# Two pairs of v times p in one TensorE visit, with five p buffers, a first softmax in halves, one W_out piece decoded later, and a new order

## The chip, the core and the metric

The kernel runs on one core of a Trainium2 chip. Its engines are TensorE (PE, with PEld for weight loads), VectorE (DVE), ScalarE (ACT), GpSimd (POOL) and SyncE (SP, which issues the DMAs); SBUF is the working memory, PSUM has eight banks of 128 x 512 words of 32 bits, which TensorE writes. The metric is the device time of one execution, in microseconds, as the median of several.

## The reference

Block-causal attention over 8 batches x 8 heads x 576 positions x 64, then a two-layer network with a gate on 4608 tokens:

```python
scores = scale * np.matmul(q, k.transpose(0, 1, 3, 2))      # q, k, v: (8, 8, 576, 64)
mask = (pos[:, None] // 64) >= (pos[None, :] // 64)
scores = np.where(mask, scores, -1000000000.0)
scores = scores - np.max(scores, axis=-1, keepdims=True)
attn = np.exp(scores)
attn = attn / (np.sum(attn, axis=-1, keepdims=True) + 1e-09)
x = np.matmul(attn, v)            # heads side by side: (4608, 512)
h = x @ w_in                      # (512, 2048)
g = h * (1.0 / (1.0 + np.exp(-h)))
out = g @ w_out                   # (2048, 512)
```

`w_in` and `w_out` arrive as 64-bit floats. q and k are scaled so that the softmax is not flat.

## The kernel before

**Precision.** A product is made of two parts of each operand, high and low, in the type fp32r: hi times hi, hi times lo and lo times hi. So every operand is split, as a rule by a cast on ScalarE (`hi`) and a subtraction on POOL (`lo`). v times p alone is in plain 32-bit floats.

**Attention.** The first two blocks of 64 queries are done apart at the start: block 0 by `First` (units a and b, four batches each) and block 1 by `Second` (c0 to c3). The other 448 queries of each head are a `Unit`, u0 to u63. A unit loads q and k, splits them (`split_hi`, `split_q`, `split_k`), makes transposed scores in three of four PSUM banks (`scores`, L702, tile S), reduces their maximum across partitions with transposing reductions (`max`, `gather`, `top`, `spread`, `wide`), subtracts it (`sub`, L745, L748, L739, tile T), takes the exponential (`exp`, into one of three p buffers), sums (`add`, `sums`), and each odd unit multiplies v and p for itself and its even mate at once, two halves of the array side by side (`pv`, L805, tile U, one PSUM bank of its own). `mult` (L809, tile xu) divides by the sums and `x_hi`, `x_lo` split the result.

**Network.** As soon as a batch's x is there, W_in's product runs in pieces (`ffn1`, L1031, tile h), whose results are kept (`keep`) and saved to DRAM (`save`). The 64 visits of `scores` and the visits of `pv` lie between these pieces. W_in's and W_out's 64-bit words are turned to 32 bits on the chip by integer operations (`rebias` on ScalarE, `sign` on POOL, `bits` on VectorE; 16 pieces w0 to w15 and o0 to o15). W_out's pieces pass in pairs through one buffer (`Turned`, t0 to t7), which forms seven combinations for a product of seven instead of eight multiplications: `x` makes sums, `hi` and `lo` split. t0 to t2 are made early and lie in a pool of their own ("ta"), t3 to t7 after the last attention unit. Then the second product goes over 18 blocks of 256 tokens with four items each (i0 to i71): `load`, `silu`, `x`, `hi`, `lo`, `prod` (L1108), and `keep`, `add` (L1143), `store` of each block's output (y0 to y17).

**Order.** No scheduler works here. A text of tokens, `ORDER`, such as `u23.pv` or `ffn`, is gone through from the first to the last, and each token's method issues its instructions to the queues of their engines, which run in that order, each instruction waiting for the semaphores of what it needs. `warm:10` issues ten matmuls of zeros.

Of the kernel before, what the change touches and what calls it, by code (L numbers as in the profile page):

```python
# [68 lines left out]
a.load b.load a.load_v w0.load b.load_v warm:10 a.scores w1.load w2.load a.max:0 a.sub:0 warm:3 b.scores c0.load a.max:1 a.sub:1  # L69
b.max:0 a.exp w3.load b.max:1 w4.load a.sum w0.rebias w0.sign w5.load b.sub:0 w6.load a.norm b.sub:1 w7.load w0.bits:0 b.exp  # L70
w0.bits:2 o1.load w1.rebias w1.sign warm:30 a.turn:0 b.sum w0.hi a.turn:1 a.back:0 w8.load w0.lo a.back:1 w1.bits:0 w2.rebias
warm:2 a.pv o0.load w1.bits:2 b.norm a.hi:0 c0.load_v a.hi:1 a.lo:0 w1.hi a.lo:1 w2.sign warm:7 b.turn:0 w3.rebias c3.load
c0.scores:0 b.back:0 b.turn:1 w5.rebias w1.lo w2.bits:0 w4.rebias ffn c0.max:0 b.back:1 w3.sign w2.bits:2 c0.exp:0 w9.load b.pv
w3.bits:0 c0.scores:1 w10.load all.mask b.hi:0 w3.bits:2 b.hi:1 ffn w2.hi c0.max:1 c3.load_v w3.hi w2.lo b.lo:0 c0.exp:1 b.lo:1
w4.bits:0 w3.lo ffn c0.sum w6.rebias c1.load w4.bits:1 w7.rebias c0.norm w4.bits:2 ffn keep w11.load w8.rebias w5.bits:0 w4.hi
save c0.turn:0 w5.bits:1 keep w4.lo c3.scores:0 w12.load c0.back:0 w5.bits:2 o1.rebias c0.turn:1 c3.max:0 w5.hi ffn save w6.bits:0
c0.back:1 w5.lo c3.exp:0 w6.bits:1 w13.load c0.pv w6.bits:2 c3.scores:1 c0.hi c1.load_v w7.bits:0 w6.hi ffn c0.lo w10.rebias
w14.load w6.lo c3.max:1 w9.rebias w7.bits:1 c3.exp:1 c1.scores:0 w7.bits:2 ffn c1.max:0 w15.load keep c3.sum c1.exp:0 save
w8.bits:0 c3.norm ffn w8.bits:1 w7.hi w8.bits:2 c1.scores:1 keep w7.lo w9.bits:0 c3.turn:0 w11.rebias save c1.max:1 w8.hi c2.load
ffn w9.bits:1 c3.back:0 w8.lo c1.exp:1 w9.bits:2 c3.turn:1 ffn w10.bits:0 c3.back:1 c1.sum w10.bits:1 w9.hi c1.norm c3.pv keep  # L80
w10.bits:2 w12.rebias ffn save w11.bits:0 w10.hi w9.lo w13.rebias w11.bits:1 c1.turn:0 o0.rebias w11.bits:2 ffn w10.lo c1.back:0
w12.bits:0 w11.hi w14.rebias c1.turn:1 w12.bits:1 w11.lo ffn c1.back:1 w12.bits:2 keep w13.bits:0 w15.rebias save c1.pv w12.hi
w13.bits:1 ffn w12.lo c1.hi c2.load_v w13.bits:2 c1.lo w13.hi c2.scores:0 w14.bits:0 keep w13.lo w14.bits:1 save ffn u0.load
c2.max:0 w14.bits:2 c2.exp:0 ffn w15.bits:0 w15.bits:1 w14.hi c2.scores:1 w15.bits:2 keep w14.lo ffn save c2.max:1 w15.hi u1.load
o0.bits:0 w15.lo all.staged c2.exp:1 ffn o0.bits:1 o0.bits:2 u0.split_hi ffn c2.sum o2.load o1.bits:0 c2.norm keep o1.bits:1
t0.hi:0 ffn save o1.bits:2 u0.split_q t0.hi:1 o3.load c2.turn:0 keep ffn u0.split_k c2.back:0 save c2.turn:1 ffn u2.load t0.x:0
c2.back:1 t0.x:1 c2.pv t0.hi:2 keep t0.x:2 u0.load_v ffn c2.hi save t0.lo:0 c3.hi u2.load_v c2.lo t0.hi:3 u3.load_v t0.lo:2 ffn
c3.lo u1.load_v t0.lo:3 u0.scores keep u0.max:0 t0.lo:1 save u0.max:1 ffn u1.split_hi u0.max:2 o2.rebias ffn u1.split_q u0.gather
o2.bits:0 o3.rebias u1.split_k u0.top ffn o2.bits:1 u0.spread u0.wide keep u3.load ffn u0.sub:0 u0.sub:1 save u0.exp:0 u1.scores
u0.sub:2 u0.exp:1 u0.exp:2 u1.max:0 ffn u1.max:1 u2.split_hi u0.add:0 u1.max:2 keep ffn u2.split_q u0.sums:0 u1.gather save  # L90
o2.bits:2 u0.add:1 u1.top ffn u1.spread o4.load o3.bits:0 u2.split_k u1.wide keep t1.hi:0 ffn u0.sums:1 save u1.sub:0 u4.load
t1.lo:0 u1.sub:1 u1.exp:0 u2.scores keep u1.sub:2 u1.exp:1 save u2.max:0 ffn u1.exp:2 u2.max:1 u3.split_hi u1.add:0 u2.max:2 u1.pv
# [344 lines left out]
def attn_ffn(ctx: ExitStack, tc: tile.TileContext, qk, v, qk0, v0, qk1, v1, w_in, w_out, out):  # L437
# [53 lines left out]
    class Weights:  # L491
# [21 lines left out]
        def rebias(u):  # L513
            if u.signed:
                u.w = bank((1, "C")[u.i])
            else:
# [1 line left out]
            nc.scalar.activation(u.w, u.word(1).bitcast(F32), AF.Copy, scale=REBIAS)
# [730 lines left out]
```

## Time and profile before

| | |
|---|---|
| three runs | 998.52, 998.63, 999.65 us; median 998.63 |
| profiled execution | 999.48 us, span of the instructions 997.8 us |
| granted TensorE clock | 1.00 in the whole span |
| busy share of the span | PE 99%, PEld 89%, DVE 77%, ACT 69%, POOL 62% |
| 16 DMA engines | 51.9% by the hardware queue |

The span is what lies between the first and the last instruction; the execution's time has 1.68 us more around it. In the rows of the trace the columns are the start, the duration, the engine, the line of the kernel, the operation, output and inputs, shape and number, and in brackets the idle time of the engine just before and what ended it. In a row of a stage they are its bounds, its length, each engine's busy time with the number of instructions in the order PE, PEld, DVE, ACT, POOL, then the granted clock, the DMA engines' share and GB/s. A matmul's duration includes the pipeline, so what it holds TensorE for is the step from its start to the next start.

### The profile page before, as it was taken

The page shows a single profiled execution, that of the slowest core. Times are in us where ns is not written, and L with a number is a line of the kernel's source. Part 1 is how long each engine was busy: PE and PEld are TensorE (multiplying, and loading weights), DVE is VectorE, ACT ScalarE, POOL GpSimd, SP SyncE. Part 2 cuts the span into 40 slices and gives each one's busy share as a digit, 9 for nine tenths or more (in the row PEclk, how much of TensorE's full clock was granted, in tenths as well). Part 3 has the DMA queues.
Part 4 walks back from the last instruction along what each step waited for, and adds up shares of the span by engine and source line. Part 5 has one row for each costly group of instructions (what it writes and reads, how often), then busy time and mean ns, then how long its engine had stood idle before and what let it go on. Part 6 is the DMA issues. An engine that isn't in the chain of part 4 may idle for free. (4 is left out here: it accounts for less than half of the span.)

```text
span 997.8 us, 20716 instructions
## 1 busy us (share of the span) xinstructions
PE 987.2 (99%) x6936; PEld 888.9 (89%) x6936; DVE 768.4 (77%) x1969; ACT 692.4 (69%) x1555; POOL 616.0 (62%) x722
## 2 busy tenths in 40 slices
PE   8999999999999999999999999999999999999998
PEld 7778787888888888888888899999999999999998
DVE  5868999988888888988888643788677666767661
ACT  4977877777777777777777555986767676666650
POOL 5677988798777777877777557654444344344430
PEclk9999999999999999999999999999999999999999
DMA  9966655545555554554555266555444544444411
GB/s 351 387 195 187 170 144 154 151 145 149 159 147 147 149 159 142 146 166 144 145 149 148 76 208 216 179 164 154 127 128 132 145 128 127 128 126 143 135 43 44
DMA packets 109803, 155.51 MB, mean 156 GB/s; under 512 B 18560, under 2 KB 83072, under 8 KB 109696
## 3 DMA queue, kind: packets, MB, share of 16 engines
q1 hardware_dynamic: 109696, 154.18, 51.9%
q8 instruction: 55, 0.90, 0.4%
q14 instruction: 52, 0.43, 0.1%
HBM read 106.95 MB, written 47.19 MB: 154 GB/s over the span
## 5 line engine op out<-in xcount | busy, mean ns | idle before, releaser
L1031 PE MATMUL h<-x,wi 128*128 128x448 f32 (+2 forms) x1968 | 422.4, 370 | 0.3 <-POOL wi L563 0.3
L1031 PEld LDWEIGHTS h<-x,wi 128*128 128x128 f32 x1968 | 357.3, 188 | 37.4 <-issue 0.9
L642 DVE TRANSPOSE_TENSOR_REDUCE Mx<-S 64x4 f32<-64x128 f32 (+4 forms) x384 | 130.4, 399 | 18.1 <-PE S L702 17.1
L755 ACT ACTIVATE p<-T 128x512 f32<-128x512 f32 (+1 forms) x192 | 114.2, 613 | 21.0 <-DVE T L745 16.1
L1037 ACT COPY g<-h 128x448 f32<-128x448 f32 (+1 forms) x160 | 86.4, 540 | 50.9 <-PE h L1031 36.0
L1096 POOL TENSOR_TENSOR x<-raw,x 128x512 fp32r<-128x512 f32 (+1 forms) x58 | 58.8, 1016 | 78.2 <-ACT x L1092 73.9
L1059 ACT ACTIVATE raw<-raw 128x1024 f32<-128x1024 f32 x72 | 76.3, 1061 | 41.7 <-DMA raw<-gdb 36.4
L1096 POOL TENSOR_TENSOR wi<-raw,wi 128x512 fp32r<-128x512 f32 (+1 forms) x56 | 56.7, 1017 | 77.6 <-ACT wi L1092 67.5
L761 POOL TENSOR_TENSOR pa<-p 128x448 f32<-128x448 f32 x64 | 73.5, 1149 | 48.4 <-ACT p L755 41.2
L683 POOL TENSOR_TENSOR qh<-qk,qh 64x576 fp32r<-64x576 f32 x64 | 91.4, 1428 | 5.0
L702 PE MATMUL S<-qh 128*128 128x448 f32 (+3 forms) x320 | 92.8, 303 | 0.0
L687 POOL TENSOR_TENSOR ql<-qk,qh 128x448 fp32r<-128x448 f32 x64 | 73.6, 1149 | 24.0 <-ACT qh L677 17.0
L677 ACT CAST qh<-qk 128x1024 fp32r<-128x1024 f32 x64 | 67.1, 1048 | 28.8 <-PE S L702 15.1
L805 PE MATMUL U<-p,v 128*64 128x448 f32 (+3 forms) x640 | 86.5, 416 | 0.0
L702 PE MATMUL S<-ql,qh 128*128 128x448 f32 (+3 forms) x320 | 83.9, 306 | 0.0
L805 PEld LDWEIGHTS U<-p,v 128*64 128x64 f32 x640 | 43.0, 137 | 42.3 <-issue 31.0
L748 DVE TENSOR_TENSOR T<-S,MR 128x384 f32<-128x384 f32 (+2 forms) x192 | 73.3, 408 | 0.0
L702 PEld LDWEIGHTS S<-ql,qh 128*128 128x128 f32 (+1 forms) x320 | 57.0, 178 | 6.5
L702 PEld LDWEIGHTS S<-qh 128*128 128x128 f32 (+1 forms) x320 | 56.8, 178 | 3.7
L764 POOL TENSOR_TENSOR pa<-pa,p 128x320 f32<-128x320 f32 x64 | 55.9, 873 | 2.5
L1096 POOL TENSOR_TENSOR gc<-raw,gc 128x512 fp32r<-128x512 f32 (+1 forms) x30 | 30.4, 1017 | 41.4 <-ACT gc L1092 33.5
L727 ACT COPY m<-m 32x14 f32<-32x14 f32 x192 | 38.7, 202 | 20.1 <-DVE m L723 18.0
(196 smaller groups left out, 2099.8 us busy)
## 6 DMA issues: line engine op xcount, KB each, us to landing
qk<-in_qk_dram SPq DMA_DIRECT2D x128, 256.0 KB, 3.8
gdb<-g SPq DMA_DIRECT2D x128, 224.0 KB, 2.3
raw<-gdb SPq DMA_DIRECT2D x64, 256.0 KB, 3.2
v<-in_v_dram SPq DMA_DIRECT2D x64, 160.0 KB, 2.3
wst<-in_moe_w_in_dram SPq DMA_DIRECT2D x16, 512.0 KB, 8.7
wst<-in_moe_w_out_dram SPq DMA_DIRECT2D x16, 512.0 KB, 4.4
gd<-g SPq DMA_DIRECT2D x32, 256.0 KB, 3.4
raw<-gd SPq DMA_DIRECT2D x32, 256.0 KB, 3.3
```

Source lines behind the costliest of these rows:

```text
L642: nc.vector.tensor_reduce(out=out, in_=in_, axis=AX.X, op=op, apply_transpose=True)
L683: nc.gpsimd.tensor_tensor(out=u.qh[r, c], in0=u.raw[r, c], in1=u.qh[r, c], op=ALU.subtract)
L687: nc.gpsimd.tensor_tensor(out=u.ql, in0=u.raw[:, :NQ], in1=u.qh[:, :NQ], op=ALU.subtract)
L702: nc.tensor.matmul(u.ps(c, w, m), u.kk[r, j * P : j * P + m], q[r, q0 : q0 + w], start=qq == 0 and not (ROWS and seg in (2, 4)), stop=qq = ...
L748: nc.vector.tensor_tensor(out=u.T[:, c + 64 : c + w], in0=u.ps(c + 64, w - 64), in1=u.mb[:, q0 + 64 : q0 + w], op=ALU.subtract)
L755: nc.scalar.activation(u.p[:, c:e], u.T[:, c:e], AF.Exp, scale=SCALE)
L761: nc.gpsimd.tensor_tensor(out=u.pa, in0=u.p[:, :NQ], in1=u.p[:, 960 : 960 + NQ], op=ALU.add)
L805: nc.tensor.matmul(U[64 * e : 64 * e + 64, q0 : q0 + w], u.vv[:, e, j], z.p[:, c : c + w], start=n == 0, stop=n == 4)
L1031: nc.tensor.matmul(o, wi[wt][:, c, w], x_of(g, c, xt), start=c + k == 0, stop=c == CT - 1 and k == 2)
L1037: nc.scalar.copy(g, hs.pop(z)[:, :n])
L1059: nc.scalar.activation(u.raw, u.raw, AF.Silu)
L1096: e.tensor_tensor(out=u.goal(1, k), in0=u.source(k), in1=u.goal(0, k), op=ALU.subtract)
```

## The change

From the ninth unit on (`u.double`), `pv` is called at every fourth unit and makes the U of the pair before the last and of the last pair, one behind the other: the first in U's bank, the second in the bank called C. Four p tiles are then alive together, and five buffers are used, two of them in a new pool. The room for them comes from "ta", which now holds t0 and t1 alone; t2 is made after the last unit like its successors. Where t2 to t7 are made, the first sum and two of four `lo` go to VectorE. A piece of W_out is decoded in place and no longer in bank C. The first block's exp, sum and norm work on halves, each of the two score banks of a and of b on its own. The whole text of the order is new; the table of score passes under `ROWS` and the options `BY_BIAS` and `RP` are not used (`ROWS` is false, the two are empty).

The first place is TensorE in the middle of attention, at one visit to `v` times `p`. S_n are the score banks, U and SC the product's banks, h the first FFN product. Before:

```order
L702 MATMUL S_4110<-qh 64x64
L702 MATMUL S_4110<-ql,qh 64x64
L805 MATMUL U<-p,v 64x448 x4
L805 MATMUL U<-p,v 64x320 x2
L805 MATMUL U<-p,v 64x192 x2
L805 MATMUL U<-p,v 64x64 x2
L1031 MATMUL h<-x,wi_78 128x448 x2
L1031 MATMUL h<-x,wi_79 128x448
```

and of the change, the unit before the visit and the one behind it:

```order
L712 MATMUL S_4090<-ql,qh 64x64
L817 MATMUL U<-p,v 64x448 x4
L817 MATMUL U<-p,v 64x320 x2
L817 MATMUL U<-p,v 64x192 x2
L817 MATMUL U<-p,v 64x64 x2
L817 MATMUL SC<-p,v 64x448 x4
L817 MATMUL SC<-p,v 64x320 x2
L817 MATMUL SC<-p,v 64x192 x2
L817 MATMUL SC<-p,v 64x64 x2
L712 MATMUL S_4174<-qh 128x448
```

Two products stand together, and the next unit's scores follow with no h between; before, three pieces of h stood there. In the whole program U is entered 32 times before and 18 times now; S is followed by h 39 times before and 49 times now.

The second place is VectorE at that same visit, from the maximum of the unit ahead of it (mj is the maximum before it is gathered, m after, MR its broadcast, Dx and dj the softmax sums). Before:

```order
L716 TENSOR_REDUCE mj<-Mx 128x14
L642 TENSOR_REDUCE Dx<-p 128x6
L642 TENSOR_REDUCE Dx<-p 128x2
L723 TENSOR_REDUCE m<-mj 32x14
L646 STREAM_TRANSPOSE MR<-m 128x448
L642 TENSOR_REDUCE Dx<-pa 128x14
L779 TENSOR_REDUCE dj<-Dx 128x28
L745 TENSOR_TENSOR T<-S_3696,MR 128x448
```

and of the change:

```order
L726 TENSOR_REDUCE mj<-Mx 128x14
L651 TENSOR_REDUCE Dx<-p 128x6
L651 TENSOR_REDUCE Dx<-p 128x2
L651 TENSOR_REDUCE Dx<-pa 128x14
L733 TENSOR_REDUCE m<-mj 32x14
L821 TENSOR_TENSOR xu<-U,MR 128x448
L790 TENSOR_REDUCE dj<-Dx 128x28
L655 STREAM_TRANSPOSE MR<-m 128x448
L755 TENSOR_TENSOR T<-S_4088,MR 128x448
```

The division of the visit's first U (the pair before the last) now stands between the maximum and its broadcast.

The third place is POOL at the start (p_288 and T are the two softmax tiles of block 0, wi_79<-wst is a sign of W_in, wi_79<-wm,wi_78 a low part). Before:

```order
L528 TENSOR_SCALAR wi_79<-wst 128x2x256
L855 TENSOR_TENSOR p_288<-p_288,rr 128x1024
L528 TENSOR_SCALAR wi_79<-wst 128x2x256
L563 TENSOR_TENSOR wi_79<-wm,wi_78 128x2x256
L855 TENSOR_TENSOR T<-T,rr 128x1024
```

and of the change:

```order
L947 TENSOR_TENSOR p_288<-p_288,rr 128x8x64 x2
L538 TENSOR_SCALAR wi_79<-wst 128x2x256 x2
L947 TENSOR_TENSOR T<-T,rr 128x8x64 x2
L538 TENSOR_SCALAR wi_79<-wst 128x2x256
L573 TENSOR_TENSOR wi_79<-wm,wi_78 128x2x256 x2
```

Both normalisations now stand ahead of W_in's first low part, each in two halves. The core of the diff, without the table of tokens:

```diff
-NTA = 3
+NTA = 2
+DOUBLE = 1
+INPLACE = 1
-LO_BY_VECTOR = ()
+LO_BY_VECTOR = (1, 3)
+X_BY_VECTOR = (0,)
...
             elif j == 0:
-                u.a = bank("C").bitcast(U32)
+                u.a = (bank("C") if u.kind == "in" or not INPLACE else u.w).bitcast(U32)
...
+            e = nc.vector if u.d >= NTA and k in X_BY_VECTOR else nc.gpsimd
...
-            e = nc.vector if k in LO_BY_VECTOR else nc.gpsimd
+            e = nc.vector if u.d >= NTA and k in LO_BY_VECTOR else nc.gpsimd
...
+            u.double = DOUBLE and i >= 8
...
             if k == 0:
-                u.p = sp.tile([P, COLS], F32, tag=f"p{u.i % 3}", name="p")
+                n = u.i % 5 if u.double else u.i % 3
+                u.p = (pools["p"] if n > 2 else sp).tile([P, COLS], F32, tag=f"p{n}", name="p")
...
         def pv(u):
-            U = u.U = pU.tile([P, 512], F32, tag="U", name="U")[:, :NQ]
-            for n, (j, c, q0, w) in enumerate(SEG[i] for i in PV):
-                for e, z in enumerate((u.mate, u)):
-                    nc.tensor.matmul(U[64 * e : 64 * e + 64, q0 : q0 + w], u.vv[:, e, j], z.p[:, c : c + w], start=n == 0, stop=n == 4)
+            for y in (units[u.i - 2], u) if u.double else (u,):
+                U = y.U = (bank("C") if u.double and y is u else pU.tile([P, 512], F32, tag="U", name="U"))[:, :NQ]
+                for n, (j, c, q0, w) in enumerate(SEG[i] for i in PV):
+                    for e, z in enumerate((y.mate, y)):
+                        nc.tensor.matmul(U[64 * e : 64 * e + 64, q0 : q0 + w], y.vv[:, e, j], z.p[:, c : c + w], start=n == 0, stop=n == 4)
...
-        def exp(u):
-            nc.scalar.activation(u.p, u.p, AF.Exp, scale=SCALE)
+        def exp(u, k):
...
+                nc.scalar.activation(u.out(k), u.out(k), AF.Exp, scale=SCALE)
...
+        def norm(u, k):
+            u.engine.tensor_tensor(out=u.out(k), in0=u.out(k), in1=u.spread(u.rr[:, k]), op=ALU.mult)
...
         def staged(u):
             pools["stage"].release()
+            pools["ta"] = tc.alloc_tile_pool(name="ta", bufs=1, side="right")
+            if DOUBLE:
+                pools["p"] = tc.alloc_tile_pool(name="p", bufs=1, side="right")
```

More of the change, by code (lines that the diff above doesn't have):

```diff
@@ L32 @@
 CT = DM // P
-NS = 4
 NX = 16
-NTA = 3
+BY_BIAS = ()
+RP = ()
+NTA = 2
+DOUBLE = 1
+INPLACE = 1
 NSLOT = 5
@@ L68 @@
 ORDER = """
[L69 to L92, printed above, removed]
@@ new lines @@
+a.exp:0 w3.load a.exp:1 a.sum:0 w4.load a.sum:1 a.norm:0 w6.load b.max:0 w5.load a.norm:1 b.max:1 w0.rebias b.sub:0 w7.load
+w0.sign warm:14 a.turn:0 b.sub:1 b.exp:0 a.turn:1 a.back:0 b.sum:0 o0.load b.exp:1 w1.sign a.back:1 w0.bits:0 w1.rebias warm:1
+a.pv o1.load b.sum:1 b.norm:0 a.hi:0 c0.load_v w1.bits:0 a.hi:1 b.norm:1 a.lo:0 w0.bits:2 warm:8 c0.scores:0 c3.load w2.sign
+w1.bits:2 w0.hi b.turn:0 c0.max:0 w2.rebias b.turn:1 w1.hi a.lo:1 w0.lo c0.exp:0 w2.bits:0 w8.load w1.lo w2.bits:2 ffn b.back:0
@@ new lines @@
+w9.load w3.sign b.back:1 w3.rebias b.pv w10.load w2.hi w3.bits:0 w4.rebias c0.scores:1 w2.lo b.hi:0 c3.load_v ffn w3.bits:2 b.hi:1
+c0.max:1 all.mask w3.hi w4.bits:0 c0.exp:1 w3.lo c1.load b.lo:0 ffn b.lo:1 w6.rebias c0.sum c3.scores:0 w11.load w4.bits:1 c0.norm
+w5.rebias w7.rebias w4.bits:2 ffn keep c3.max:0 w12.load w4.hi w5.bits:0 save c3.exp:0 w4.lo c0.turn:0 w5.bits:1 ffn w5.bits:2
+c0.back:0 w6.bits:0 w13.load w5.hi c0.turn:1 w6.bits:1 keep w5.lo c3.scores:1 c0.back:1 save w6.bits:2 w8.rebias c0.pv c3.max:1
@@ new lines @@
+w14.load w6.hi w9.rebias w7.bits:0 w6.lo ffn c1.load_v c3.exp:1 w7.bits:1 w7.bits:2 ffn c0.hi c3.sum w15.load w8.bits:0 w7.hi
+c3.norm ffn keep c0.lo w10.rebias save w8.bits:1 w11.rebias c3.turn:0 w7.lo w8.bits:2 keep c1.scores:0 w9.bits:0 c3.back:0 save
+w8.hi c3.turn:1 w9.bits:1 w12.rebias w8.lo c1.max:0 ffn c3.back:1 w9.bits:2 c1.exp:0 w10.bits:0 c3.pv w10.bits:1 w9.hi c1.scores:1
+w10.bits:2 w13.rebias w9.lo ffn o0.rebias c1.max:1 c2.load w10.hi w11.bits:0 c1.exp:1 w10.lo o0.bits:0 ffn w11.bits:1 keep c1.sum
@@ new lines @@
+keep w15.hi ffn save c2.max:1 u1.load w15.lo all.staged t0.hi:0 t0.hi:1 c2.exp:1 ffn t0.lo:0 t0.lo:1 u0.split_hi c2.sum ffn
+c2.norm keep o2.rebias ffn save o3.rebias o2.bits:0 t0.hi:3 u0.split_q o3.bits:0 c2.turn:0 keep ffn o2.bits:1 c2.back:0 save
+u0.split_k o3.bits:1 t0.hi:2 o2.bits:2 c2.turn:1 ffn o3.bits:2 u2.load c2.back:1 t0.lo:3 t1.hi:0 t1.hi:1 c2.pv t1.lo:0 keep save
+t1.lo:1 ffn c2.hi u0.load_v c3.hi u2.load_v c2.lo t0.lo:2 u3.load_v c3.lo u0.scores u1.load_v u0.max:0 t1.x:0 u0.max:1 ffn
@@ L690, in scores @@
         def scores(u):
-            banks = [bank((3 * u.i + k) % NS) for k in range(3)]
+            banks = [bank((0, 1, 2, 3, "C")[(3 * u.i + k) % NS]) for k in range(3)]
             def ps(c, w, r=P):
```

628 lines of the change are left out of this document (326 added, 302 removed).

## The prediction

> **What bounds the kernel now.** I read the page's busy shares and slices first, then the table by stages, then TensorE's waits, then TensorE's instructions in order of time. In these rows S is the scores tile (L702), U the product of v and p (L805), h the first FFN product (L1031), and L1108 the second FFN product.
>
> ```profile
> span 997.8 us, 20716 instructions
> PE 987.2 (99%) x6936; PEld 888.9 (89%) x6936; DVE 768.4 (77%) x1969; ACT 692.4 (69%) x1555; POOL 616.0 (62%) x722
> 100.00:575.00 475.00, 475.00 (x2671) 398.45 (x2670) 416.89 (x1233) 344.99 (x867) 369.61 (x478) 1.00 0.51 147
> 575.00:625.00 50.00, 50.00 (x249) 46.33 (x248) 20.78 (x30) 29.25 (x53) 34.32 (x34) 1.00 0.64 204
> 627.00:993.40 366.40, 364.38 (x3030) 362.63 (x3028) 254.03 (x554) 243.25 (x447) 145.63 (x144) 1.00 0.44 127
> PE S L1108 <- DVE g L1143: 1.6, 3, 0.7
> ```
>
> TensorE is busy for all of 100 to 575 us (attention with the first product) and all of 575 to 625 us, at a granted clock of 1.00; in the second product it lacks 366.40 - 364.38 = 2.02 us, mostly in three waits for the output sums of L1143. VectorE, the next, has 416.89 of 475 us, 88%. So from 100 us on only what TensorE itself does sets the time: fewer or shorter matmuls, or less lost between them. Busy time hides the second, since matmul ends are modelled; it shows in the starts.
>
> **The change part by part. Two pairs of v times p at once.** The matmuls stay the same; the number of visits to U falls from 32 to 18. What a visit costs beside its matmuls is read from starts, first S to U to h, then S straight to h:
>
> ```profile
> 304.07 0.36 PE L702 MATMUL S<-ql,qh 128*128 128x448 f32 x1
> 304.27 0.19 PE L702 MATMUL S<-qh 128*64 128x64 f32 x1
> 304.30 0.22 PE L702 MATMUL S<-ql,qh 128*64 128x64 f32 x1
> 304.45 0.60 PE L805 MATMUL U<-p,v 128*64 128x448 f32 x2
> 304.88 0.55 PE L805 MATMUL U<-p,v 128*64 128x448 f32 x2
> 305.25 0.55 PE L805 MATMUL U<-p,v 128*64 128x448 f32 x2
> 306.87 0.28 PE L805 MATMUL U<-p,v 128*64 128x64 f32 x4
> 306.92 0.23 PE L805 MATMUL U<-p,v 128*64 128x64 f32 x2
> 307.08 0.47 PE L1031 MATMUL h<-x,wi 128*128 128x448 f32 x1
> 307.39 0.36 PE L1031 MATMUL h<-x,wi 128*128 128x448 f32 x1
> 307.59 0.37 PE L1031 MATMUL h<-x,wi 128*128 128x448 f32 x1
> 312.23 0.19 PE L702 MATMUL S<-qh 128*64 128x64 f32 x1
> 312.26 0.22 PE L702 MATMUL S<-ql,qh 128*64 128x64 f32 x1
> 312.31 0.45 PE L1031 MATMUL h<-x,wi 128*128 128x448 f32 x1
> 312.60 0.56 PE L1031 MATMUL h<-x,wi 128*128 128x448 f32 x2
> ```
>
> Going in: the second 64-column S starts 0.03 us after the first, but U starts 0.15 after it, 0.12 more; U's first pair takes 0.43 (304.45 to 304.88) where the next takes 0.37, 0.05 to 0.06 more, of which I take 0.05. In: 0.17. Going out: U's last 64-column pair holds 0.16 (306.92 to 307.08) where the pair ahead holds 0.05 (306.87 to 306.92), 0.10 more; the first h holds 0.31 where the next holds 0.20, 0.10 more. Out: 0.20. S straight to h: 0.05 instead of 0.03, and the first h 0.29 instead of 0.20: 0.10. None of these has a wait in the trace.
>
> From the order I count the changes. Visits to U: 32 before, 18 now, so 14 times in and out fall away: 14 x (0.17 + 0.20) = 5.2 us. S straight to h: 39 before, 49 now, since some visits stood between the two: 10 x 0.10 = 1.0 us comes back. The gain is **4.2 us**. (The few visits that h leads into, or S follows, are priced the same.)
>
> New is the step from one U to the next inside a visit, 14 times, here SC after U. No row has it. Below, it costs nothing, as between pieces of one U; a gain is excluded, since the matmuls are the same. Above, it costs the start and end of a visit without its neighbours, 0.05 + 0.10 = 0.15. I take 0.05, because both sides have the same shape and type and only the weights' lead is short after the 64-column pieces: 14 x 0.05 = **0.7 us** back, 0 to 2.1.
>
> **The tight spots.** Nine of the doubled visits have no h behind them: S, two U, S. The next S starts 1.36 (S, 302.94 to 304.30) + 0.15 + 2 x 2.63 (304.45 to 307.08) + 0.13 = 6.9 us after the last one, where it was 7.95 (302.94 to 310.89). What must be ready by then, in the same kind of place before:
>
> ```profile
> 302.94 0.36 PE L702 MATMUL S<-qh 128*128 128x448 f32 x1
> 303.55 2.03 DVE L642 TRANSPOSE_TENSOR_REDUCE Mx<-S 128x14 f32<-128x448 f32 x6
> 304.68 1.04 ACT L677 CAST qh<-qk 128x1024 fp32r<-128x1024 f32 x1 [0.19 <-ACT g L1037]
> 307.13 0.23 DVE L723 TENSOR_REDUCE m<-mj 32x14 f32<-32x56 f32 x1
> 307.41 1.43 POOL L683 TENSOR_TENSOR qh<-qk,qh 64x576 fp32r<-64x576 f32 x1
> 308.06 0.65 DVE L646 STREAM_TRANSPOSE MR<-m 128x448 f32<-128x448 f32 x1 [0.69 <-ACT m L727]
> 308.74 0.62 DVE L745 TENSOR_TENSOR T<-S,MR 128x448 f32<-128x448 f32 x1
> 309.81 0.27 DVE L739 TENSOR_TENSOR T<-S,MR 64x128 f32<-64x128 f32 x1
> 310.89 0.37 PE L702 MATMUL S<-qh 128*128 128x448 f32 x1
> 314.66 0.62 DVE L809 TENSOR_TENSOR xu<-U,MR 128x448 f32<-128x448 f32 x1
> ```
>
> The operands qh are ready at 307.41 + 1.43 = 308.84, 5.9 us after S began: 1.0 us to spare. The first bank of S that is used again is free at 308.74 + 0.62 = 309.36, 6.4 us after, and wanted after two passes of about 0.20, at 7.3: 0.9 to spare. The second is free at 309.81 + 0.27 = 310.08, 7.14 us after, wanted by the seventh of the next S's ten passes, at about 7.8: 0.66 to spare. The order puts one xu (0.62) among these, but between m and MR, where VectorE waited 0.69 us for ScalarE anyway; the U that it reads is the visit's first, whose last matmul starts by 307.08, ahead of m's 307.13. I take 0; below nothing is to be had, since TensorE waits nowhere there; above see the first rival. The same cover hides the fifth p buffer and U's use of bank C.
>
> **First block's softmax in halves, and the new loads.** The order has the two normalisations ahead of the first sign on POOL, and the second pair's q and k, then all v, ahead of W_in's first piece.
>
> ```profile
> 9.14 1.13 PE L906 MATMUL S<-qk 64*64 64x64 f32 x32 [0.16 <-DMA qk<-in_qk_dram]
> 10.00:20.00 10.00, 9.57 (x162) 8.79 (x154) 8.50 (x15) 5.98 (x10) 7.38 (x5) 1.00 1.04 392
> 12.56 0.64 ACT L518 ACTIVATE S<-wst 128x512 f32<-128x512 f32 x1 [1.84 <-DMA wst<-in_moe_w_in_dram]
> 14.11 1.90 POOL L855 TENSOR_TENSOR p<-p,rr 128x1024 f32<-128x1024 f32 x1
> 22.71 1.67 PE L1031 MATMUL h<-x,wi 128*128 128x256 f32 x12
> ```
>
> The transfers run at 392 GB/s there, so 2 x 256 KB of v ahead of b's scores and of W_in's first piece move each about 0.52 MB / 392 GB/s = 1.3 us later: b's scores from 9.14 to 10.5, the piece from 12.56 to 13.9. Block 0's normalisation, which had stood behind the sign until 14.11, is done by about 13. But ScalarE's copy of the turned p now stands behind that piece's rebias and b's exp: 13.9 + 0.64 + two halves of exp. So the first block's v times p comes about 0.7 us earlier at best, and the weights 1.3 us later at worst. The first h at 22.71 needs both. I take **0**, -0.7 to +1.3. The 43 warming matmuls instead of 52 fill idle time only.
>
> **One W_out piece later, and work moved to VectorE.** Six of eight transposed pieces are now made after the last U, not five.
>
> ```profile
> 575.23 0.69 DVE L541 TENSOR_SCALAR SC<-wraw 128x512 uint32<-128x512 uint32 x1 [3.54 <-ACT wraw L518]
> 581.78 1.28 POOL L635 TENSOR_TENSOR tb<-xs,tb 128x512 fp32r<-128x512 f32 x1
> 615.18 0.69 DVE L541 TENSOR_SCALAR SC<-wraw 128x512 uint32<-128x512 uint32 x1 [4.93 <-ACT wraw L518]
> ```
>
> From the first to the fifth piece is 39.95 us, 10.0 each, one behind the other through one buffer. Of each, three POOL steps of about 1.28 go to VectorE, priced at its 0.69 for the same elements: 10.0 - 1.8 = 8.2, six take 49 us where five took 50. VectorE has 50 - 20.78 = 29 us free there and gains 6 x 2.1 + one piece's 4.2 = 17. The last piece is first read by the fourth of the second product's 72 items, 3 x 366.4 / 72 = 15 us after its start. That is the cover: 0. Were it gone, each us of lateness beyond it costs one. In the second product only the order differs: 0, with the 2.02 us it lacks gone below, and twice as much again, +4, above.
>
> **The sum.** 4.2 - 0.7 = 3.5 us less. The profiled execution took 999.48 with a span of 997.8; it becomes 996.0 and 994.3. Against the median of the runs, 998.63, which is 0.85 below the profiled one, it is **995.1 us**. About 0.2% (2.0 us) is what a measurement can tell from no change, so faster is below 996.6 and slower above 1000.6.
>
> **The rivals.**
>
> First, slower: *the wait moves to the tight spots.* If ScalarE's three m copies stand behind the whole cast of qh (1.04) and one more cast of about half its width (0.5), the second bank is 1.54 us late; 0.66 is spare, so TensorE waits 0.88 at nine places: 995.1 + 7.9 = 1003.0. It decides from 0.66 us of lateness on, and makes the kernel slower from about 1.3. For it: 88% VectorE and a gap 1 us shorter. Against: the rows' reserves, and xu in the idle slot. Chance 0.11.
>
> Second, *a switch is paid per change between 64-column and 128-column weights, whoever uses them.* Every S ends in 64 columns, so a visit to U after S would add no change. Runs of 64 columns followed by others go from 39 + 32 = 71 to 49 + 18 = 67, and arrivals at U from h from 7 to 3: at 0.20 and 0.17 this is 1.5 us, 997.1. For it: U and the last two S share the shape 128*64. Against: S itself goes from 128 to 64 columns at no price (304.07 to 304.27, 0.20, like h), and leaving U costs twice what leaving S does. [...] Chance 0.05.
>
> Third, *the gain is given back at the ends*: the start comes out at +1.3 and the second product loses some 1.7 us more at L1143: 998.1. For it: these sums wait behind other VectorE work already, and every item is reordered. Against: the work is the same. Chance 0.12.
>
> Fourth, *the new order also clears the second product's waits*: 995.1 - 2.0 = 993.1. Chance 0.10.
>
> **How the numbers follow.** My forecast has 0.62, 995.1, its own range 992.5 to 997.5 by the step between two U and the start; 0.57 of it lies below 996.6. Faster: 0.57 + 0.10 = 0.67. Same: 0.05 + 0.05 + 0.10 of the third = 0.20. Slower: 0.11 + 0.02 of the third at its upper bound = 0.13. The range goes from 992.0 (no price between two U, the start at -0.7, the waits of the second product gone: 991.7) to 999.5, which takes in the second and third rivals.
>
> **What would show it.** Right: 18 visits to U, those of 40 matmul records taking about 5.3 us; TensorE busy for all of attention; the last U about 3.5 us earlier, less any shift at the start; waits at L1143 near 2 us. Wrong: waits of S for VectorE's T or POOL's qh at doubled visits (first rival); the second product starting no earlier than before although no wait shows, so the steps in and out were not saved (second); a first h well after 22.7 us, or TensorE idle for 4 us and more after it starts the second product (third).

## The result, and the profile after

The changed kernel takes **1014.47 us** (median of five runs, 1013.27 to 1017.06) where the kernel before, in five runs beside it, takes 999.12 (998.52 to 999.68): a ratio of 1.0158, with a 95% interval of 1.0142 to 1.0175. It is 1.6% slower; forecast were 995.1 us. The profiled execution took 1017.06 us with a span of 1015.4.

The busy shares of the kernel after, and its stages as in the rows shown of before (bounds, length, busy time of PE, PEld, DVE, ACT and POOL with the number of instructions, granted clock, DMA share, GB/s):

```profile
span 1015.4 us, 20670 instructions
...
PE 987.6 (97%) x6918; PEld 889.8 (88%) x6918; DVE 782.9 (77%) x1993; ACT 686.3 (68%) x1557; POOL 596.2 (59%) x706
```

```profile
40.00:100.00 60.00, 54.07 (x392) 43.87 (x391) 46.03 (x82) 41.77 (x107) 42.25 (x34) 0.97 0.57 186
100.00:575.00 475.00, 475.00 (x2708) 400.38 (x2707) 422.30 (x1252) 347.00 (x871) 362.88 (x472) 1.00 0.53 150
575.00:625.00 50.00, 49.79 (x243) 45.09 (x243) 33.51 (x50) 28.26 (x54) 21.59 (x23) 1.00 0.64 204
631.00:1011.00 380.00, 369.97 (x3031) 367.23 (x3029) 250.96 (x555) 238.24 (x448) 144.17 (x144) 0.99 0.42 122
```

Of before, the one of these stages that the prediction had not shown:

```profile
40.00:100.00 60.00, 60.00 (x441) 48.85 (x441) 47.71 (x104) 46.50 (x122) 42.11 (x35) 1.00 0.71 222
```

TensorE is full through attention, as before. But it now lacks 60 - 54.07 = 5.9 us between 40 and 100 us, where it lacked nothing, and 380 - 369.97 = 10.0 us in the second product, where it lacked 2.0. In both places the granted clock is below 1.00 (0.97 and 0.99). TensorE's waits in the kernel after say for whom (waited for, us in total, times, longest); the first is the second product's, the other four lie between 44 and 95 us:

```profile
PE S L1133 <- DVE g L1168: 9.5, 8, 2.6
PE S L712 <- DVE x L1036: 2.2, 1, 2.2
...
PE S L1028 <- ACT MR L877: 1.4, 1, 1.4
PE S L997 <- DVE x L1036: 1.3, 1, 1.3
...
PE S L874 <- POOL MR L867: 1.0, 1, 1.0
```

To see where the time went I cut the profiled spans of before, after and all experiments at the same points of the program, by TensorE's starts: the first step of h behind the 96th, the first scores of the ninth unit (u8), the last matmul of U, and the first of the second product. The stages hold the same matmuls in both programs, with two exceptions besides the warming matmuls at the start. Eight transposes (L862, 0.8 us by starts) lie ahead of the first cut in before, e4, e6, e8 and e11 to e13, and behind it in the others. And e6_split has six h steps (1.2 us) in attention that the others have in the next stage. (The table is worked out from the starts of the profiled executions; the one of after was the slowest of its five, 2.6 us above their median. The experiments follow below.)

| us | past 96th h | to ninth unit | attention, to last U | to second product | second product | span |
|---|---|---|---|---|---|---|
| before | 53.44 | 83.21 | 430.25 | 59.83 | 371.04 | 997.77 |
| **after** | 52.34 | 92.01 | 424.94 | 61.67 | 384.39 | 1015.35 |
| e1_bankC | 52.56 | 86.68 | 424.95 | 61.45 | 382.73 | 1008.37 |
| e2_second_old | 51.95 | 90.51 | 424.94 | 61.83 | 370.01 | 999.24 |
| e3_both | 52.07 | 86.64 | 424.95 | 60.39 | 370.00 | 994.05 |
| e4_ends_old | 53.28 | 83.20 | 424.94 | 60.01 | 371.69 | 993.12 |
| e5_keep_first | 52.41 | 91.96 | 424.94 | 60.75 | 387.32 | 1017.38 |
| e6_split | 53.98 | 83.21 | 435.11 | 59.01 | 372.18 | 1003.49 |
| e7_pieces | 52.20 | 86.44 | 424.95 | 60.44 | 370.00 | 994.03 |
| e8_keep | 53.57 | 83.17 | 424.94 | 60.01 | 372.61 | 994.30 |
| e9_early_hi | 52.26 | 90.40 | 424.95 | 61.07 | 371.68 | 1000.36 |
| e11_head | 54.88 | 83.19 | 424.95 | 60.27 | 370.22 | 993.51 |
| e12_pool | 53.53 | 83.21 | 424.94 | 65.23 | 370.88 | 997.79 |
| e13_regular | 53.48 | 83.20 | 424.94 | 60.40 | 369.75 | 991.77 |

Before against after: -1.1 at the start, +8.8 up to the ninth unit (-0.3 and +8.0 without the eight transposes), **-5.3 in attention**, +1.8 to the second product, **+13.4 in the second product**: +17.6. The part that the prediction spent most words on did what it said. Two stages that it had put at nothing, or almost, cost some 21 us. (Of the 1.8 to the second product the runs say little: bank C alone leaves 1.6 of it and the old second order alone 2.0, both together 0.6.)

### The profile page after: what moved, and what is told of

Same layout as the page of the kernel before. It is cut to its first block, busy times and chain, and to the rows that moved or that the text cites. A ratio compares the mean times of both kernels' runs of the same rounds, so it can differ in the third digit from the quotient of the medians.

```text
span 1015.4 us, 20670 instructions
## 1 busy us (share of the span) xinstructions
PE 987.6 (97%) x6918; PEld 889.8 (88%) x6918; DVE 782.9 (77%) x1993; ACT 686.3 (68%) x1557; POOL 596.2 (59%) x706
## 5 line engine op out<-in xcount | busy, mean ns | idle before, releaser
L1084 ACT ACTIVATE raw<-raw 128x1024 f32<-128x1024 f32 x72 | 76.4, 1061 | 71.4 <-DMA raw<-gdb 66.3
L758 DVE TENSOR_TENSOR T<-S,MR 128x256 f32<-128x256 f32 (+2 forms) x192 | 73.3, 409 | 0.0
L1133 PE MATMUL S<-tb,x 128*128 128x256 f32 x450 | 59.1, 283 | 0.2 <-DVE x L1121 0.2
L1133 PEld LDWEIGHTS S<-tb,x 128*128 128x128 f32 x450 | 56.2, 192 | 0.4 <-DVE x L1121 0.4
L655 DVE STREAM_TRANSPOSE MR<-m 128x448 f32<-128x448 f32 x64 | 40.3, 630 | 16.5 <-ACT m L737 15.6
```

Of the source, the lines that this page charges most:

```text
L758: nc.vector.tensor_tensor(out=u.T[:, c + 64 : c + w], in0=u.ps(c + 64, w - 64), in1=u.mb[:, q0 + 64 : q0 + w], op=ALU.subtract)
L1084: nc.scalar.activation(u.raw, u.raw, AF.Silu)
L1133: nc.tensor.matmul(o, quarter(u.g[a], j)[:, P * e : P * e + P], quarter(turned[d].g[b], TORDER[FACTOR[pr]]), start=u.q == 0 and i % 2 == 0 ...
```

## The experiments

The two theories with which the experiments began: up to the ninth unit, W_out's decode in place is stretched on VectorE beside GpSimd; in the second product, ScalarE's copy of an output sum stands behind a silu that waits for its DMA. Of the first, the rows in the kernel after. L551, L555 and L561 are the three steps of a piece; `wraw` is SBUF, `SC` is bank C of PSUM, which W_in's pieces still use (the last row). VectorE, then GpSimd:

```profile
49.43 1.36 DVE L551 TENSOR_SCALAR wraw<-wraw 128x512 uint32<-128x512 uint32 x1
...
52.17 2.15 DVE L555 SCALAR_TENSOR_TENSOR wraw<-wst,wraw 128x512 uint32<-128x512 uint32 x1
...
54.84 1.19 DVE L561 SCALAR_TENSOR_TENSOR wraw<-wst,wraw 128x512 uint32<-128x512 uint32 x1
...
57.34 0.42 DVE L551 TENSOR_SCALAR wraw<-wraw 128x512 uint32<-128x512 uint32 x1
...
58.27 1.69 DVE L555 SCALAR_TENSOR_TENSOR wraw<-wst,wraw 128x512 uint32<-128x512 uint32 x1
...
60.48 0.68 DVE L561 SCALAR_TENSOR_TENSOR wraw<-wst,wraw 128x512 uint32<-128x512 uint32 x1
...
63.78 0.69 DVE L561 SCALAR_TENSOR_TENSOR wm<-wst,SC 128x512 uint32<-128x512 uint32 x1
```

```profile
49.21 1.29 POOL L573 TENSOR_TENSOR wi<-wm,wi 128x512 fp32r<-128x512 f32 x1 [0.36 <-ACT wi L570]
51.87 1.90 POOL L867 TENSOR_TENSOR MR<-MR,rr 128x1024 f32<-128x1024 f32 x1 [1.37 <-ACT wm L528]
53.73 1.75 POOL L573 TENSOR_TENSOR wi<-wm,wi 128x512 fp32r<-128x512 f32 x1
58.15 1.26 POOL L573 TENSOR_TENSOR wi<-wm,wi 128x512 fp32r<-128x512 f32 x1 [2.67 <-ACT wi L570]
```

The two steps on `wraw` that no GpSimd instruction overlaps take 0.42 and 0.68. The others on `wraw` end a fixed time after GpSimd's: 51.87 + 1.90 = 53.77, and VectorE's step ends at 54.32, 0.55 later; 53.73 + 1.75 = 55.48 and 56.03, 0.55; 58.15 + 1.26 = 59.41 and 59.96, 0.55; L551 at 50.79, 0.29 after 50.50. Most of the step's 0.68 (or 0.42) was still to be done when GpSimd's instruction ended, so VectorE stood meanwhile. This holds for the whole kernel: of its 32 decode steps with both inputs in SBUF, the eight that begin while a GpSimd instruction runs take 1.17 to 2.15 us and all end 0.55 us after it; the other 24, one of which begins 1 ns behind GpSimd's, take 0.68 to 0.69. The 12 steps with one input from PSUM that begin beside GpSimd take 0.68 to 0.70. One is the last row, beside a GpSimd instruction from 63.28 to 64.56. L551 in place has one input from SBUF and is stretched too, to 1.36 us in the first row; alone it takes 0.42 us, where its form with bank C takes 0.68.

### Bank C again

```diff
-INPLACE = 1
+INPLACE = 0
...
-o2.bits:0 t0.hi:3 u0.split_q o3.bits:0 c2.turn:0 keep ffn o2.bits:1 c2.back:0 save u0.split_k o3.bits:1 t0.hi:2 o2.bits:2 c2.turn:1 ffn o3.bits:2
+o2.bits:0 t0.hi:3 u0.split_q o2.bits:1 c2.turn:0 keep ffn o2.bits:2 c2.back:0 save u0.split_k o3.bits:0 t0.hi:2 o3.bits:1 c2.turn:1 ffn o3.bits:2
...
```

> The changed kernel with W_out's pieces decoded in bank C of PSUM again, as before, and no longer in place in SBUF; since two pieces can't share that bank, the three steps of a piece stand before those of the next, in the places that decode steps have in the order. Theory: in place, VectorE's decode steps are stretched beside GpSimd (eight of them took 1.2 to 2.1 us in the trace of after, where bank C gave 0.69), some 6 us of VectorE between 50 and 85 us, where it is full, and TensorE waited 5.9 us there and then ran 3.4 us at half clock. So 5 to 7.5 us less than 1014.5: 1007 to 1009.5, and TensorE waits under 1.5 us between 44 and 95 us. Rival: the new order alone is at fault, since it asks for four decoded pieces and two transposed ones before the second attention unit; then the bank changes nothing: 1013 to 1016, with the same waits.

Measured: 1009.23 us (1007.85 to 1010.84) beside 998.24 for before; ratio 1.0102, 1.0085 to 1.0120. The stage to the ninth unit fell from 92.01 to 86.68. VectorE's steps in this kernel, by group (busy us, mean ns), and TensorE's waits between 44 and 92 us:

```profile
L555 DVE SCALAR_TENSOR_TENSOR SC<-wst,SC 128x512 uint32<-128x512 uint32 x11 | 7.6, 695 | 0.3
...
L551 DVE TENSOR_SCALAR SC<-wraw 128x512 uint32<-128x512 uint32 x4 | 2.8, 690 | 1.7 <-ACT wraw L528 1.5
```

```profile
PE S L997 <- DVE x L1036: 1.3, 1, 1.3
PE S L874 <- POOL MR L867: 1.0, 1, 1.0
```

No step is stretched now, and 5.3 us are gone: the in-place decode cost that much. (Since bank C holds one piece at a time, the edit also puts the three steps of a piece together; no run separates the two.) Of it some 1.7 us, half of 3.41, are the clock: in the kernel after, the granted clock is 0.50 for 3.41 us from 83.89 on, behind the 2.2 us wait. Rows of after by windows:

```profile
83.89:87.30 3.41, 3.41 (x13) 2.96 (x13) 2.56 (x8) 0.48 (x1) 2.48 (x3) 0.50 0.72 194
87.30:90.72 3.41, 3.41 (x17) 2.81 (x16) 0.43 (x3) 2.88 (x9) 2.61 (x3) 1.00 0.21 79
```

Of the 8.8 us, 3.5 remain (86.68 against 83.21), 0.8 of them the eight transposes, with two waits of the second block's units, 2.3 us, left. So both are partly right: the bank for the larger share, the order for the rest.

### The second product in its old order

Every step from the first `i0.load` on, put in the order of before:

```diff
-i31.prod:0 i35.lo:3 i38.silu i31.prod:1 i35.lo:2 i31.prod:2 y7.keep i36.hi:0 y7.add:0 i31.prod:3
+i31.prod:0 i35.lo:3 i35.hi:1 i37.x:0 i35.lo:1 i31.prod:1 y7.keep i37.x:2 i38.silu i37.x:1 i31.prod:2 i39.load y7.add:0 i37.x:3 i31.prod:3
...
```

> The changed kernel, but from the second product's first load on, the remaining steps stand in the order of before; all else as changed. Theory: the second product's 13.4 us of loss come from its order, by which ScalarE's copy of an output sum (y.keep) stands behind a silu that waits for its DMA; with the old order the waits for L1168 fall from about 10 us to under 2.5 us and the half-clock stretch at 800 us is gone: 1000 to 1002.5. Rival: the loss is not in the order but in what the second product meets (last W_out pieces late, other buffers): 1011 to 1015.

Measured: 1000.0 us (998.47 to 1001.86); ratio 1.0013, 1.0002 to 1.0023. The second product takes 370.01, 14.4 less than after and 1.0 less than before. (In e1_bankC, with the order of the change and no half-clock stretch in this stage, it takes 382.73, still 11.7 more than before.) Nothing but the order costs here: the late W_out pieces, the buffers and VectorE's new work are all still in it.

### Both, and the doubled visits alone

e3_both is the two edits together. e4_ends_old has besides the order of before up to the ninth unit's scores:

```diff
-(the steps of the change up to u8.scores)
+(the same steps in the order of before: a.exp:0 a.exp:1 for a.exp, and so on; o4, o5 and t2 not among them)
```

> Both edits together: bank C for the decode and the old order of the second product, on the changed kernel. If both theories hold and the losses add up, 1014.5 - 13 - 6 = 995.5, 994 to 997.5. If the start's order is at fault by itself, 1000 to 1002.5; if only the decode theory holds, 1007 to 1009.5.

> The doubled visits alone: the order of before up to the ninth unit's scores (without t2 and the pieces o4 and o5, which are made behind the last unit as in the change, and with the first softmax's halves side by side), the changed attention from there, the old order of the second product, and bank C for the decode. Theory: the prediction's own sum holds for this part, 4.2 us less of switching less 0.7: 995.1, 993.5 to 996.5, with TensorE without waits from 100 to 575 us. Rival: what attention gained in the trace of after (5 us from the third unit to the second product) is only TensorE working off h that the start's waits had pushed behind; then 998 to 1000.

Measured: e3_both 995.77 us (995.04 to 995.88), ratio 0.9965, 0.9952 to 0.9978; e4_ends_old **994.90** us (994.78 to 995.84), ratio 0.9961, 0.9948 to 0.9975. The losses of e1 and e2 add up, and what is left of the change gains what was forecast for the whole. In e4 the second stage is 83.20, before's own; in e3, and in e1, it is 3.4 longer, against 1.4 less ahead of the cut in e3. The transposes count in both; at the ninth unit e3 is 2.1 us behind before, and that is what the order of the start costs by itself. TensorE's waits in e3_both, 24 to 140 us, are those of the second block's units (L996 and L873 there, after's L997 and L874); the first and the third, 2.3 us, lie in that stage. e4_ends_old has 0.3 us in all:

```profile
PE S L996 <- DVE x L1035: 1.3, 1, 1.3
PE S L996 <- DVE wm L560: 1.2, 1, 1.2
PE S L873 <- POOL MR L866: 1.0, 1, 1.0
```

The rival that attention's gain was only postponed work falls: with a start that is level with before's, attention still takes 5.3 us less.

### The copy ahead of the silu

The second product's waits, followed back in the kernel after. ScalarE between 789 and 801 us, with its idle time in brackets:

```profile
789.33 0.40 ACT L1117 CAST wi<-raw 128x256 fp32r<-128x256 f32 x1
...
796.57 1.06 ACT L1084 ACTIVATE raw<-raw 128x1024 f32<-128x1024 f32 x1 [4.07 <-DMA raw<-gdb]
797.53 1.05 ACT L1117 CAST gc<-h 128x512 fp32r<-128x512 f32 x2
799.46 1.06 ACT L1084 ACTIVATE raw<-raw 128x1024 f32<-128x1024 f32 x1 [0.87 <-DMA raw<-gdb]
800.42 0.35 ACT L1158 COPY s<-S 128x256 f32<-128x256 f32 x1
```

The last row is `y7.keep`; ahead of it stand two silus that had waited 4.07 and 0.87 us for their loads. VectorE's sum and TensorE's next block follow at once:

```profile
800.80 0.42 DVE L1168 TENSOR_TENSOR g<-S,s 128x256 f32<-128x256 f32 x1 [1.39 <-ACT s L1158]
```

```profile
801.28 2.29 PE L1133 MATMUL S<-ta,wi 128*128 128x256 f32 x9 [2.62 <-DVE g L1168]
```

So I first blamed the place of the copy:

```diff
-i31.prod:0 i35.lo:3 i38.silu i31.prod:1 i35.lo:2 i31.prod:2 y7.keep i36.hi:0
+i31.prod:0 i35.lo:3 y7.keep i38.silu i31.prod:1 i35.lo:2 i31.prod:2 i36.hi:0
...
```

> The changed kernel with one thing moved: where a silu stands between the last item's first product (prod:0) of a block and the copy of that block's output sum (y.keep) on ScalarE, the copy goes ahead of the silu; 13 of 18 blocks. The silus, the loads and the buffers stay late as they are. Theory: the output sums wait because y.keep stands behind a silu that waits for its DMA; the waits for L1168 fall from some 10 us to under 3 us, and without a wait over 2 us the half-clock stretch at 800 us is gone too: 1014.5 - 7 - 3.4 = 1004, 1001 to 1006.5. Rival: late silus hurt by themselves, through the operands that are made from them and through VectorE's adds behind these; then moving the copies does little: 1011 to 1015.

Measured: **1018.16** us (1015.94 to 1022.45), ratio 1.0202, 1.0181 to 1.0224. Not better, and rather worse. The second product's waits in this kernel:

```profile
PE S L1133 <- ACT s L1158: 9.6, 8, 4.2
PE S L1133 <- DVE g L1168: 2.1, 3, 1.1
```

The waits for the sums fell from 9.5 to 2.1, as the theory had it, but waits for the copy itself took their place: the second product of the item writes the bank that the copy reads, so a copy ahead of it holds it up. Of the 13 copies moved, eight do so: five by 0.46 us, the others by 0.7, 2.35 and, at item 31, 4.2, because an earlier silu still stood waiting. ScalarE was late as a whole, not this one copy. The theory fell.

### The last readers of a buffer

What makes a silu's load late is in the same rows. The load goes into the buffer of the item four earlier, and SP issues it when that item's last reader, `lo:1` on GpSimd, is through; that one needs `hi:1`, the 789.33 row (item 33). SP's wait between 780 and 802 us in the kernel after, and the same `hi:1` in the kernel before:

```profile
SPq L1081 <- POOL wi L1121: 7.6, 1, 7.6
```

```profile
776.55 0.41 ACT L1092 CAST wi<-raw 128x256 fp32r<-128x256 f32 x1
```

Item 29's product starts at 776.47 in before and 783.39 in after; its `hi:1` comes 0.1 us behind in the one and 5.9 behind in the other. In the order of before nearly every `hi:1` stands directly behind the first product of the item four earlier. In the new order 13 stand up to three products later, and 24 `lo:1` with them or apart. Three products are 2.2 us; the rest of the 5.9 is ScalarE's waiting in silus. Moved up:

```diff
-i29.prod:0 i33.lo:3 i35.x:0 i36.silu i29.prod:1 i35.x:2 i35.x:1 i29.prod:2 i34.hi:0 i35.x:3 i35.x:4 i29.prod:3 i33.hi:1 i34.lo:0 i29.prod:4 i29.prod:5 i33.lo:1
+i29.prod:0 i33.hi:1 i33.lo:1 i33.lo:3 i35.x:0 i36.silu i29.prod:1 i35.x:2 i35.x:1 i29.prod:2 i34.hi:0 i35.x:3 i35.x:4 i29.prod:3 i34.lo:0 i29.prod:4 i29.prod:5
...
```

> The changed kernel with the last two readings of an item's raw buffer (hi:1 on ScalarE, lo:1 on GpSimd) moved up to directly behind the first product of the item four earlier, where the order of before has nearly all of them; 13 hi:1 and 24 lo:1 from item 12 on. The copies y.keep, the silus and the loads stand as in the change. Theory, formed after e5_keep_first: the loss is in a ring. A late hi:1 or lo:1 frees the raw buffer late, its next load and with it the silu comes late, ScalarE waits in that silu and what stands behind it (the next hi:1, y.keep) is late again. Then the waits of the second product fall from 11 us to about 4 us and the half-clock stretch goes: 1014.5 - 7 - 3.4 = 1004, 1001.5 to 1007. Rival: the places of y.keep and of the sums set the waits, as in the first theory, and the ring has slack: 1011 to 1016.

Measured: **1001.70** us (1000.80 to 1003.03), ratio 1.0031, 1.0020 to 1.0041; 12.8 us less than after, from the places of 37 instructions. The second product takes 371.68. Its waits and ScalarE's silus (L1083 there), and that silu wait in after and in before:

```profile
PE S L1132 <- DVE g L1167: 1.5, 2, 0.9
```

```profile
ACT raw L1083 <- DMA raw<-gdb: 29.2, 32, 2.7
```

```profile
ACT raw L1084 <- DMA raw<-gdb: 66.3, 40, 4.1
```

```profile
ACT raw L1059 <- DMA raw<-gdb: 36.4, 26, 3.1
```

ScalarE's time in these waits is large where the loss is: 36.4 in before, 66.3 in after, 29.2 here. It is a ring: a late last reader makes a late load, a late silu, and behind it on ScalarE the next late last reader. (The half-clock stretch of 6.83 us at 800.69 in after, some 3.4 us, went too, as expected. The gain is more than expected mainly since TensorE's waits in this stage fell from 10.0 to 1.8 us and not to 4.)

### The rest of the second product

Both ideas again, the copy ahead of the silu (e8_keep) and the ring (e13_regular), on e4_ends_old, which in its profile still waited 1.2 us at item 44:

```diff
 (e4_ends_old)
 i43.prod:0 i47.lo:3 i47.hi:1 i50.silu i47.lo:1 i43.prod:1 i43.prod:2 i51.load i48.hi:0 y10.keep
 (e8_keep)
 i43.prod:0 i47.lo:3 i47.hi:1 y10.keep i50.silu i47.lo:1 i43.prod:1 i43.prod:2 i51.load i48.hi:0
 (e13_regular, with three hi:1 and nine lo:1 moved up besides)
 i43.prod:0 i47.lo:3 i47.hi:1 i47.lo:1 i43.prod:1 y10.keep i50.silu i43.prod:2 i51.load i48.hi:0
```

> The kernel of e4_ends_old with five of its y.keep moved ahead of the silu before them, in blocks 0, 5, 8, 10 and 13. Theory: the wait of 1.2 us at the item 44 (its third product, for L1167) goes, the rest stays: 993.7, 993 to 994.4. Rival: that wait has another cause: 994.5 to 995.5.

> The kernel of e4_ends_old with the ring of the second product put in order throughout: in the blocks 5, 8, 10 and 13 y.keep and then the silu stand directly behind the last item's second product, and the five hi:1 and seven more lo:1 that still stood late are moved up as in e9_early_hi. Theory: the ring is what makes the waits, so the remaining 1.2 us at item 44 and most of the 0.5 us at items 12 and 16 go: 993.6, 992.8 to 994.4. Rival: what is left comes from the sums' adds on VectorE, behind other work: 994.5 to 995.5.

Measured: e8_keep 996.55 us (995.72 to 997.29), ratio 0.9980, 0.9971 to 0.9989: three of the five copies ahead of the second product hold it up by 0.46 us, as in e5_keep_first. e13_regular **993.57** us (993.24 to 994.01), ratio 0.9947, 0.9933 to 0.9960, the fastest of all: 0.53% less than before. Its second product takes 369.75 and waits 0.2 us for a sum:

```profile
PE S L1132 <- DVE gc L1120: 0.2, 1, 0.2
PE S L1132 <- DVE g L1167: 0.2, 1, 0.2
```

That the ring's repair gained this is not shown. The interval overlaps that of e4_ends_old, 0.9948 to 0.9975. And with the order of e4_ends_old unchanged, the second product of the other six kernels that have it (e2, e3, e6, e7, e11, e12) takes 370.00 to 372.18 us, with 0.2 to 0.9 us of waiting at item 44.

### The price of a visit

One piece of h put between the two U of each doubled visit of e4_ends_old:

```diff
-            for y in (units[u.i - 2], u) if u.double else (u,):
+            for y in ((units[u.i - 2], u)[k],) if u.double else (u,):
...
-u20.max:1 u19.pv u21.split_hi u20.max:2
+u20.max:1 u19.pv:0 ffn u19.pv:1 u21.split_hi u20.max:2
...
```

> The kernel of e4_ends_old with each of the 14 doubled visits split again: one piece of h stands between the two U, taken from the place behind the visit. Buffers, other orders and work are the same. Theory: a visit's price is what the prediction said, 0.17 in and 0.20 out; by the steps seen in the trace of e4_ends_old, 0.15 within U, 0.09 from h into U and 0.10 from U into h, 0.34. So 14 x 0.34 to 0.37 = 4.8 to 5.2 us more: 994.9 becomes 999.4 to 1000.4. Rival: the gain of e4_ends_old came from elsewhere in the attention's new order, for instance h steps of 0.2025 instead of 0.2065 us, and a visit costs little: under 997.5.

Measured: 1005.06 us (1003.29 to 1005.60), ratio 1.0061, 1.0048 to 1.0073; attention 435.11, 10.2 more than e4_ends_old. Of these, by starts, 5.0 are the visits as priced: all U but the last take 81.59 instead of 79.50, and the 14 split pieces of six h steps 1.424 each instead of 6 x 0.2025, 2.9 together. Another 1.2 are the six h steps that e4_ends_old has in the next stage. The remaining 4 are not a visit's price. Scores became longer, by 3.0 us in all and up to 2.13 us where 1.41 is usual, with waits of which the profile names

```profile
PE S L712 <- POOL qh L693: 0.7, 2, 0.4
```

The h that went into the visit was missing behind it, between one unit's scores and the next. That is the first rival's mechanism, a reserve used up, in a kernel that took the cover away; in the change itself it doesn't occur. Not all of the 4 us is explained.

### The start

e7_pieces keeps the new start but puts W_out's first pieces where before has them; e11_head takes only the first block's order:

```diff
 (e7_pieces, against e3_both)
-save o3.rebias o2.bits:0 t0.hi:3 u0.split_q
+u0.gather o2.bits:0 o3.rebias save u1.split_k
...
 (e11_head, against e4_ends_old)
-a.load b.load a.load_v w0.load b.load_v warm:10 a.scores
+a.load a.load_v b.load b.load_v w0.load warm:10 a.scores
...
```

> The kernel of e4_ends_old, but with the new order of the start, in which only the steps of W_out's pieces o0 to o3 and of t0 and t1 stand where the order of before has them, behind the same neighbours. Theory: the new start is about 1 us faster up to 52 us, and its loss from there to the second unit comes from the early W_out pieces, which fill VectorE: then 994.9 - 1.0 = 993.9, 993 to 994.7, without waits of TensorE between 44 and 95 us. Rival: the new order of the second block's units (c0 to c3) is itself at fault: 995.5 to 998, with the waits of L997 and L874 still there.

> The kernel of e4_ends_old with the new order of the first block alone, from the first load to the second v times p of that block (softmax in halves, the new loads, the normalisations ahead of the signs, 43 warming matmuls); the rest of the start as before. Theory: the head gains what the trace of after shows at the 48th step of h, 0.7 to 1.1 us, and it was the order of the second block's units that gave it back in e7_pieces: 993.9, 993.2 to 994.6. Rival: the steps behind the head can't follow it, and the waits come there: 994.8 to 996.

Measured: e7_pieces 996.09 us (995.61 to 997.70), ratio 0.9976, 0.9966 to 0.9986; e11_head 995.22 (994.56 to 996.49), 0.9965, 0.9953 to 0.9978. In e7 the stage to the ninth unit is 86.44, as in e3 with its early pieces, so with bank C the pieces' place is not what costs; the order of the second block and the first units is. Its waits there:

```profile
PE S L711 <- DVE T L754: 1.3, 2, 1.1
PE S L996 <- DMA qk<-in_qk_dram: 0.8, 1, 0.8
PE S L873 <- POOL p L866: 0.2, 1, 0.2
```

Only the first of them lies in that stage, 1.3 of its 3.2 us; 0.8 are the eight transposes, and some 1 us is open. e11 tells nothing for the new head: it is level with e4. Its first cut is 1.6 later (54.88), with 3.41 us at half clock ahead of its first h, which e4 had as well.

### The work moved to VectorE

```diff
-LO_BY_VECTOR = (1, 3)
+LO_BY_VECTOR = ()
-X_BY_VECTOR = (0,)
+X_BY_VECTOR = ()
```

> The kernel of e4_ends_old with the first sum and the two low parts of t2 to t7 back on GpSimd. Theory: a W_out piece pair takes 10.2 us instead of 9.2, so the last low part lands 6 us later, still some 8 us ahead of its first reader: no change, 994.5 to 995.5. Rival: ScalarE's and VectorE's steps for the first items of the second product stand behind the late pieces in their queues, so the product starts later: 996.5 to 1001.

Measured: 998.95 us (997.99 to 1000.14), ratio 1.0004, 0.9995 to 1.0012; 4 us more than e4_ends_old. TensorE's waits between 570 and 630 us, and that stage in e12_pool and in e4_ends_old:

```profile
PE h L1055 <- ACT g L1061: 4.0, 5, 1.3
```

```profile
570.00:621.00 51.00, 47.03 (x227) 41.89 (x226) 21.06 (x31) 25.64 (x50) 37.07 (x36) 1.00 0.62 195
```

```profile
570.00:621.00 51.00, 51.00 (x252) 46.96 (x251) 32.74 (x48) 31.39 (x57) 22.93 (x24) 1.00 0.66 217
```

With GpSimd's steps late, ScalarE waits in its casts, and the copies of h (L1061) stand behind these: h has no free bank. So six pieces after the last unit cost nothing only because VectorE took its share.

## Why the prediction was wrong

**The switches: right, and somewhat too low.** A doubled visit in the kernel after, from the scores ahead of it to the scores behind:

```profile
295.88 0.22 PE L712 MATMUL S<-ql,qh 128*64 128x64 f32 x1
296.03 0.60 PE L817 MATMUL U<-p,v 128*64 128x448 f32 x2
```

```profile
298.56 0.55 PE L817 MATMUL SC<-p,v 128*64 128x448 f32 x2
```

```profile
301.15 0.47 PE L712 MATMUL S<-qh 128*128 128x448 f32 x1
```

It goes in at 0.15, as before, and takes 301.15 - 296.03 = 5.12 us, where two single ones take 2 x 2.63 = 5.26. The step from U to SC costs nothing: 0.05 from the last pair, as inside U. So the 0.7 us that I gave back there were not due, and its lower bound was right. By starts, from the first U to the second product, e4_ends_old against before: U 2.1 less, S 0.8, h 2.3, together 5.1, where the sum without the 0.7 had 4.2. The rest may sit in the h steps (below). The rival of a price per change of columns falls: attention gained 5.3 us, not 1.5.

**The tight spots: right.** Attention is busy for 475.00 of 475 us; the nine spots wait nowhere.

**The start: right for the first h steps, wrong in where it stopped.** The first h came at 21.04 instead of 22.71, past the lower bound of -0.7, but it lies anywhere from 20.98 to 23.02 in the kernels with this start (below). The first cut comes 1.1 us earlier, and 0.3 earlier without the transposes that now stand behind it, which is within the bounds. But I took the first h for the end of that part. Behind it comes the new order of the second block and the first units, and I had looked at none of its rows: with bank C, the new start is 2.0 to 2.1 us behind before at the ninth unit (e7_pieces, e3_both).

**The decode in place: not priced at all.** In the step on W_out's pieces I counted the instructions that go to VectorE, and left out that those which were there already now read `wraw` instead of bank C. It cost 5.3 us (e1_bankC). The rows of before held only the 0.69 with bank C, so no row of it gave the price.

**One piece later: the 0 was right, the reasons only in part.** With t2 to t7 the pairs come every 9.2 us (ScalarE's first copy of the first pair at 571.53 and of the sixth at 617.63 in after), not 8.2. The cover that I named, the first reader in the second product, is not the one that ends first: without VectorE's share it was ScalarE's copies of h that came late, and 4 us were lost (e12_pool).

**"In the second product only the order differs: 0", +4 above: wrong, and the largest error.** It cost 13.4 us, some 3 of them by the half-clock stretch. I took equal work for equal time because the stage was 99% busy. But its order holds a ring of four raw buffers, and the new order lengthens it at 13 places (e9_early_hi). The third rival had both places, the start and L1143, at a chance of 0.12, but priced the second at 1.7 us, and the +4 was twice the 2.02 that the stage lacked. What a stage lacks now is no bound for what another order can cost it.

## What to carry to other kernels

Where an order is written anew, go through every ring of buffers in it and look at the last reader: if it stands later against the work that it paces, all of the ring is later, and the engine that stands waiting in its own queue drags unrelated work along, as ScalarE did here, with 66.3 us of waits in its silus instead of 36.4. Equal work and a busy engine say nothing on that. When an operand moves from PSUM to SBUF, look at what GpSimd does at that time (here eight of 32 steps took 1.17 to 2.15 us instead of 0.68); and read a change of many parts by stages that hold the same work, since here a real gain of 5 us lay hidden under losses of some 21.
